# Matmuls without use behind the stages of batch 0's front end, a fold that takes high parts first, and sums of batch 1 queued behind it

## The chip, the cores and the metric

The kernel runs on one core of a Trainium2 chip. A core has TensorE (PE, matmuls; its weight loads are shown as PEld), VectorE (DVE), ScalarE (ACT), GpSimdE (POOL) and SyncE (SP, which issues most of the transfers); each works through its own queue in order and waits for the others by semaphores. The metric is the device time of one execution in microseconds. The kernel before took 1105.98 us (median of 3 runs, 1105.55 to 1107.51).

## The reference

Eight batches, each with 8 heads, 576 tokens and 64 channels a head, go through attention against keys and values that are averaged over 8 tokens each, and then through a mixing block: a Fourier transform over tokens and channels whose real part is added, a normalisation, and a two-layer network with 2048 hidden channels. Cut to what matters:

```python
k_p = k.reshape(B, H, Sp, 8, D).mean(axis=3)
v_p = v.reshape(B, H, Sp, 8, D).mean(axis=3)
attn = softmax((q @ k_p.T) / sqrt(D))          # per batch and head
x = (attn @ v_p).transpose(0, 2, 1, 3).reshape(B, S, H * D)
mixed = np.real(np.fft.fft(np.fft.fft(x, axis=1), axis=2))
u = x + mixed
un = (u - mean(u)) / sqrt(var(u) + 1e-06)
out = u + np.maximum(un @ w_ch1, 0.0) @ w_ch2
```

## The kernel before

For each batch `b` the generator `fe(b)` (L231 to L656) makes the front end: attention, transform and normalisation. `ffn` (L661) makes the two-layer network for a block of columns. Most precise products are made of three: a value is split into a high part and a low part, and high times high, low times high and high times low are added in PSUM.

**Batch 0's front end, in order.** Head pairs are taken in the order 3, 2, 0, 1. For a pair `g`: sums of the keys (L259 on VectorE for batch 0), copies of them into `kpb` (L268, L269), scores into PSUM tiles `psS` (L327, three column groups and then two), maximum and subtraction on VectorE (L329, L338), exponential on ScalarE (L340), sum and reciprocal on VectorE (L341 to L343), the product with it on GpSimd (L344). Then come transposes into `psT`, `psV` and `psR` (L365, L375, L376, L386), copies out of them on ScalarE (L368, L380, L390), and the values `psX` (L408). For pairs 3 and 2 ScalarE copies psX to `X` (L410 to L415); for pairs 0 and 1 VectorE adds and subtracts it (L418, L419).

**The transform.** The even channels are folded on VectorE to `tmpE` (L484), ScalarE rounds that to the high part `eh` (L477), and VectorE subtracts to get the low part `el` (L478; both are shown as `f`). One row is folded apart: GpSimd writes `xt` (L490), ScalarE its high part into `xe` (L493), VectorE its low part (L494). The odd channels give `tmpO` (L496). Then come three products `psA` (L517), each of seven records: `eh` by the high constants twice, `el` by the high constants twice, `eh` by the low constants twice, and `xe`. They are copied out in two parts (L501, L502 and L505 to L523). `psB` (L533, eighteen records) does the same for the odd channels; `psQ` and `psP` (L550) transform over the tokens; L556 to L583 add the results on VectorE; `psM` (L596) gives the mean that L600 subtracts; L590 and L591 split the outcome into `unh` and `unl`, the operands of the first FFN product `g` (L687).

**PSUM.** There are eight banks: `g1` and `fe` with two each, `acc0` to `acc3`. `bank` (L217) gives batch 0 the banks of the FFN, in turn g1, acc0, g1, acc1, acc2, acc3; the other batches use `fe`. The FFN takes g1 for its first product and acc0 to acc3 for its second.

**Weights.** They come as pieces of 512 KB (numbers 0 to 33, the last four half as large; the first 24 are w1 and w2 in turn). `prep_w` (L175) makes a piece's high part (`wd`, then L199) and its low part (L200), on ScalarE (L190, L192), VectorE (L194, L195), ScalarE and GpSimd; the low part is written to DRAM (L201) and read again for each FFN step (L210). When a piece is prepared, the place in which it lay takes the load of a later one (L202). Piece 4's first ScalarE operations are queued behind batch 0's last copy of `psB` (L189).

**Order.** The program is traced in the order of the generators (L707 on): batch 0's front end up to the mark "z", eleven weight pieces, batch 1 with the rest of batch 0 and the first steps of batch 2, then FFN blocks with the other batches between. A scheduler with a timing model then fixes each engine's queue; what it takes to be ready sooner stands further ahead. So batch 1's and the weights' operations stand between batch 0's in every queue. `tc.issue_after(ins)` queues what its block traces on the engine of `ins` behind `ins`; it is an order of issue, not a wait. Buffers have tags with a number of slots: `k` (one slot) holds batch 1's keys of one pair, and also `xt`; `v` and `vs` hold batch 1's values of one pair and their sums; `w` (seven slots) the weights in work and the low parts.

Of the kernel before, what the change touches and what calls it, by code (L numbers as in the profile page):

```python
# [8 lines left out]
F32 = mybir.dt.float32  # L9
# [5 lines left out]
ALU = mybir.AluOpType  # L15
# [7 lines left out]
P = 128  # L23
# [29 lines left out]

TAIL0, TAIL1, NEXT, STEPS = 10, 11, 20, 10
E0, O0, E1, O1 = 0, 1, 2, 3

HEADS = [(0, 1), (2, 3), (5, 4), (7, 6)]
GROUPS = [(3, 2), (0, 1)]
# [17 lines left out]
def raw(ap):  # L76
    return ap.bitcast(F32)
# [3 lines left out]
def tile_kernel(ctx: ExitStack, tc: tile.TileContext, qt, kt, vm, vr, w1, w2, cad, cbd, mkd, out):  # L81
# [93 lines left out]
    def prep_w(n):  # L175
        if n >= len(pieces):
            return
        i, f, c, w, _ = pieces[n]
        cl = slice(c * P, (c + w) * P)
        if wide:  # L180
            st = staged.pop(n)
            hi = st[:, :, :, 1]
            halves = st.bitcast(U16)
            d0 = wk.tile([P, DM], I32, tag="w", bufs=7, name="wd")[:, 0:w * P]
            di = d0.rearrange("p (c m) -> p c m", m=P)
            dh = d0.bitcast(U16).rearrange("p (c m h) -> p c m h", m=P, h=2)
            d0 = d0.bitcast(F32)

            with tc.issue_after(behind["B", 0].ins) if n == 4 else ExitStack():  # L189
                nc.scalar.activation(hi.bitcast(F32), hi.bitcast(F32), AF.Copy, scale=REBIAS)  # L190

                nc.scalar.activation(dh[:, :, :, 0], st.bitcast(U8)[:, :, :, 3], AF.Copy, scale=1.0 / 32.0, bias=-15.5 / 32.0)  # L192

            nc.vector.tensor_scalar(out=dh[:, :, :, 1], in0=halves[:, :, :, 3], scalar1=0x8000, scalar2=None, op0=ALU.bitwise_and)  # L194
            nc.vector.scalar_tensor_tensor(out=di, in0=hi, scalar=3, in1=di, op0=ALU.logical_shift_left, op1=ALU.bitwise_or)  # L195
        else:
            d0 = staged.pop(n)
        wh = high(i, f)[:, cl]
        nc.scalar.copy(out=wh, in_=d0)  # L199
        nc.gpsimd.tensor_tensor(out=d0, in0=d0, in1=raw(wh), op=ALU.subtract)  # L200
        nc.sync.dma_start(wls[i][:, f, cl], d0)  # L201
        for m in after.get(n, ()):  # L202
            load_w(m)
# [10 lines left out]

    turn, behind = [0], {}

    def bank(b, name, late=False):  # L217
        tag = "fe"
        if b == 0 and not late:
            tag = ["g1", "acc0", "g1", "acc1", "acc2", "acc3"][turn[0] % 6]  # L220
            turn[0] += 1
        return pp.tile([P, 512], F32, tag=tag, bufs=2 if tag in ("fe", "g1") else 1, name=name)

# [2 lines left out]

    def tt(name, dt=F32):
        return wk.tile([P, 5 * W2J], dt, tag="t", bufs=2, name=name)


    def fe(b):  # L231
# [24 lines left out]
        def total(out, src, pool):  # L256

            if b not in pool:
                nc.vector.tensor_reduce(out=out, in_=src, op=ALU.add, axis=AX.X)  # L259
                return  # L260
            for n in (4, 2, 1):
                nc.gpsimd.tensor_tensor(out=out if n == 1 else src[:, :, 0:n], in0=src[:, :, 0] if n == 1 else src[:, :, 0:n], in1=src[:, :, 1] if n == 1 else src[:, :, n:2 * n], op=ALU.add)  # L262
# [49 lines left out]
        def scores(gi, i):  # L312
# [10 lines left out]
            for c0, n in ((0, 3), (3, 2)):  # L323
                ps = bank(b, f"psS{b}_{g}_{c0}")
                for c in range(n):
                    r0 = SROW[c0 + c]
                    nc.tensor.matmul(ps[:, c * W2J:(c + 1) * W2J], lhsT=q[:, r0:r0 + P], rhs=kpb[g % 2], start=True, stop=True)  # L327
                pv = ps[:, 0:n * W2J].rearrange("p (c h j) -> p c h j", h=2, j=J)
                nc.vector.tensor_reduce(out=mx[:, c0:c0 + n], in_=pv, op=ALU.max, axis=AX.X, negate=(b, g) in SM)  # L329
                if (b, g) in SM:  # L330
                    nm = mx[:, c0:c0 + n]
                    nc.vector.tensor_scalar(out=nm, in0=nm, scalar1=1.0 / 64.0, scalar2=None, op0=ALU.mult)
                    for c in range(n):
                        for h in range(2):
                            x = (slice(None), c0 + c, slice(h, h + 1))
                            nc.scalar.activation(t[:, c0 + c, h], pv[:, c, h], AF.Exp, scale=1.0 / 64.0, bias=mx[x], accum_out=sm[x])
                else:
                    nc.vector.tensor_tensor(out=t[:, c0:c0 + n], in0=pv, in1=mx[:, c0:c0 + n].unsqueeze(3).broadcast_to([P, n, 2, J]), op=ALU.subtract)  # L338
# [17 lines left out]
        def transposes(gi):  # L356
# [3 lines left out]
            for i, g in enumerate(pairs):  # L360
                t = st["t", g]
                ah, al = gt(2 * i, "ah"), gt(2 * i + 1, "al")
                ps = bank(b, f"psT{b}_{g}")
                for c in range(4):
                    nc.tensor.transpose(out=ps[:, c * P:(c + 1) * P], in_=t[:, c, 0:P], identity=ident)  # L365
                if b in NAT:
                    ah = raw(ah)
                nc.scalar.copy(out=ah[:, 0:512], in_=ps)  # L368
                if b not in NAT:
                    nc.vector.tensor_tensor(out=al[:, 0:512], in0=ps, in1=raw(ah[:, 0:512]), op=ALU.subtract)  # L370
                a[g] = (ah, al)
# [11 lines left out]
            rem = [(512, S, ps[0:32, 2 * P + 64:3 * P])]  # L383
            ps2 = bank(b, f"psR{b}_{gi}")
            for c in range(4):
                nc.tensor.transpose(out=ps2[0:32, c * P:(c + 1) * P], in_=rt[:, c], identity=ident)  # L386
            rem.append((0, 512, ps2[0:32, :]))
            for a0, a1, src in rem:
                if b in NAT:
                    nc.scalar.copy(out=raw(R[0:32, a0:a1]), in_=src)  # L390
# [7 lines left out]
        def values(g):  # L398
            ah, al = st["a"][g]
            wh, wl = st["w", g]  # L400
            for cl in halves:
# [3 lines left out]
                else:  # L405
                    mm = [(wh, ah[:, cl]), (wl, ah[:, cl]), (wh, al[:, cl]), (rw[g in (1, 2)], st["R"][0:96, cl])]
                for i, (w, a) in enumerate(mm):
                    nc.tensor.matmul(ps, lhsT=w, rhs=a, start=(i == 0), stop=(i == len(mm) - 1))  # L408
                if g == 3:
                    nc.scalar.copy(out=Xb[:, O0, cl], in_=ps)  # L410
                    nc.scalar.copy(out=Xb[0:1, E1, cl], in_=ps[0:1])
# [63 lines left out]
        def split(dst, src, n):  # L475
            eh, el = [gt(i, "f").rearrange("p (g s) -> p g s", g=2)[:, :, 0:n] for i in dst]
            nc.scalar.copy(out=eh, in_=src)  # L477
            eng.tensor_tensor(out=el, in0=src, in1=raw(eh), op=ALU.subtract)  # L478
            return eh, el

        Xe = Xb.rearrange("p (g t) s -> p t g s", t=2)
# [9 lines left out]
        nc.scalar.copy(out=xt[:, 0:HS + 1:HS], in_=o0[:, 0:S:HS])  # L491
        nc.scalar.copy(out=xt[:, HS + 1:HS + 2], in_=o0[:, HS:HS + 1])
        nc.scalar.copy(out=xe[0:1], in_=xt)  # L493
        nc.vector.tensor_tensor(out=xe[32:33], in0=xt, in1=raw(xe[0:1]), op=ALU.subtract)  # L494
        tmp = tt("tmpO").rearrange("p (g s) -> p g s", g=2)[:, :, 0:HS]
        behind["O", b] = (nc.vector if b == 0 else nc.gpsimd).tensor_tensor(out=tmp, in0=Ov[:, :, 0:HS], in1=Ov[:, :, HS:S], op=ALU.subtract)  # L496
        yield
# [10 lines left out]

        AB = [gt(0, "A0"), gt(1, "A1"), None, None, gt(4, "AB2")]
        A2, B2 = AB[4][:, 0:258], AB[4][:, 258:514]  # L510
        for i, m in enumerate((P, P, 34)):
            s0 = i * P
            ps = bank(b, f"psA{b}_{i}")[0:m, 0:258]
            mm = [(x[:, j, s0:s0 + m], cc[:, j, y]) for x, y in ((eh, 0), (el, 0), (eh, 1)) for j in range(2)]
            mm.append((xe[:, s0:s0 + m], xc))
            for n, (w, a) in enumerate(mm):
                nc.tensor.matmul(ps, lhsT=w, rhs=a, start=(n == 0), stop=(n == len(mm) - 1))  # L517
            if i < 2:
                parts((AB[i],), ps, 258)
            else:  # L520
# [72 lines left out]
        for cl in halves:  # L593
            ps = bank(b, f"psM{b}")[:, 0:HS]
            if b in NM:
                nc.tensor.matmul(ps, lhsT=raw(avg), rhs=s_[:, cl], start=True, stop=True)  # L596
            else:
                nc.tensor.matmul(ps, lhsT=avg, rhs=sh[:, cl], start=True, stop=False)
                nc.tensor.matmul(ps, lhsT=avg, rhs=sl[:, cl], start=False, stop=True)
# [288 lines left out]
```

## Time and profile before

| | |
|---|---|
| runs shown | 1105.98 us median, 1105.55 to 1107.51 |
| profiled execution, its own time | 1103.99 us |
| its span, first to last instruction | 1102.2 us |
| mean granted TensorE clock | 0.978 |
| TensorE busy | 1048.4 us (95%) |
| VectorE busy | 615.1 us (56%) |
| ScalarE busy | 415.6 us (38%) |
| GpSimd busy | 249.6 us (23%) |
| moved by DMA | 175.79 MB, mean 159 GB/s |

Times in the profile are microseconds from the span's start. A row of the timeline gives start, length, engine, line of the kernel, operation, written and read tiles, shapes, and how many records it merges; in brackets stands how long the engine stood idle before it, and what ended that. A merged row's length reaches to the end of its last record, which overlaps the next row, so what a matmul costs is read from one start to the next. A float32 product leaves two records, a product of rounded parts one. The page's forty slices give each engine's busy share in tenths. Seven tenths of the chain of work that ended last are the FFN's two products:

```profile
PE acc L671 35%; PE g L687 35%; PE psX L408 3%; PE psS L327 2%; PE psA L517 2%; PE psP L550 2%; PE psB L533 1%; PE psQ L550 1%; PE psT L365 1%; DMA k<-in_kt 1%; DMA wst<-in_w 1%; DVE unl L591 1%; DVE acc L701 0%; PE psR L386 0%; DVE X L600 0%
```

### The profile page before, as it was taken

The numbers are of one execution on the slowest core, as the hardware profiler recorded it, in microseconds if no ns is written. First come the engines' busy times: TensorE is split into PE (matmuls) and PEld (weight loads), VectorE is DVE, ScalarE is ACT, GpSimd is POOL, SyncE is SP. The second block draws the span as 40 slices with busy tenths as digits, with TensorE's granted clock in tenths as the row PEclk, the third lists the DMA queues.
The fourth block names the chain that finished last, engine by engine and source line by source line (L and its number), as shares of the span: only waits on it lengthen the run. The fifth ranks groups of instructions, "written<-read, shape, count | busy, mean of one in ns | idle before, by whom it ended". The sixth has DMA issues, their size and how long they took to land.

```text
span 1102.2 us, 17441 instructions
## 1 busy us (share of the span) xinstructions
PE 1048.4 (95%) x6484; PEld 1009.0 (92%) x6484; DVE 615.1 (56%) x1237; ACT 415.6 (38%) x1102; POOL 249.6 (23%) x249
## 2 busy tenths in 40 slices
PE   6659988999999999999999999999998999999997
PEld 5447878999999999999999999999997999999997
DVE  7597877845386464754467454755547544532122
ACT  5678754443144331533324332433314422221110
POOL 4463355212140032200331111500323000400000
PEclk9768999999999999999999999999999999999999
DMA  6759977655345454444534444435534334346563
GB/s 219 266 185 304 314 256 226 202 175 172 115 118 157 134 162 126 126 140 153 155 110 137 146 139 147 131 113 172 161 95 127 96 106 125 106 124 186 167 186 98
DMA packets 91877, 175.79 MB, mean 159 GB/s; under 512 B 10128, under 2 KB 17296, under 8 KB 91536
## 3 DMA queue, kind: packets, MB, share of 16 engines
q1 hardware_dynamic: 91504, 172.01, 50.8%
q0 software_dynamic: 288, 2.66, 0.6%
q8 instruction: 51, 0.84, 0.3%
q14 instruction: 34, 0.28, 0.1%
HBM read 156.81 MB, written 17.83 MB: 158 GB/s over the span
## 4 chain that ended last, share of the span: by engine, by line
PE 83%; DVE 4%; DMA 2%; ACT 1%; issue 1%; POOL 1%; SPq 0%; DVEq 0%; POOLq 0%; ACTq 0%
PE acc L671 35%; PE g L687 35%; PE psX L408 3%; PE psS L327 2%; PE psA L517 2%; PE psP L550 2%; PE psB L533 1%; PE psQ L550 1%; PE psT L365 1%; DMA k<-in_kt 1%; DMA wst<-in_w 1%; DVE unl L591 1%; DVE acc L701 0%; PE psR L386 0%; DVE X L600 0%
## 5 line engine op out<-in xcount | busy, mean ns | idle before, releaser
L692 DVE SCALAR_TENSOR_TENSOR hl<-g,hh 128x384 fp32r<-128x384 f32 (+1 forms) x208 | 108.5, 522 | 209.9 <-ACT hh L691 208.8
L691 ACT ACTIVATE hh<-g 128x384 fp32r<-128x384 f32 (+1 forms) x208 | 96.5, 464 | 325.6 <-PE g L687 313.8
L671 PE MATMUL acc<-hh,w2h 128*128 128x384 f32 (+1 forms) x832 | 190.2, 329 | 3.4 <-ACT hh L691 2.8
L671 PE MATMUL acc<-hh,w2low 128*128 128x384 f32 (+1 forms) x832 | 186.5, 326 | 0.1
L671 PE MATMUL acc<-hl,w2h 128*128 128x384 f32 (+1 forms) x832 | 181.5, 327 | 2.8 <-DVE hl L692 2.8
L687 PE MATMUL g<-unh,w1low 128*128 128x384 f32 (+1 forms) x832 | 179.0, 330 | 2.8 <-DMA w1low<-w1l 2.7
L687 PE MATMUL g<-unl,w1h 128*128 128x384 f32 (+1 forms) x832 | 177.6, 330 | 3.8 <-DVE unl L591 3.4
L687 PE MATMUL g<-unh,w1h 128*128 128x384 f32 (+1 forms) x832 | 175.9, 329 | 2.7 <-ACT unh L590 2.7
L671 PEld LDWEIGHTS acc<-hh,w2h 128*128 128x128 f32 x832 | 142.6, 189 | 5.9 <-ACT hh L691 3.7
L687 PEld LDWEIGHTS g<-unl,w1h 128*128 128x128 f32 x832 | 141.6, 191 | 6.5 <-DVE unl L591 5.0
L687 PEld LDWEIGHTS g<-unh,w1low 128*128 128x128 f32 x832 | 141.0, 191 | 5.3 <-DMA w1low<-w1l 4.0
L687 PEld LDWEIGHTS g<-unh,w1h 128*128 128x128 f32 x832 | 139.9, 190 | 5.6 <-ACT unh L590 4.0
L671 PEld LDWEIGHTS acc<-hl,w2h 128*128 128x128 f32 x832 | 140.8, 189 | 4.2 <-DVE hl L692 3.5
L671 PEld LDWEIGHTS acc<-hh,w2low 128*128 128x128 f32 x832 | 143.4, 188 | 0.6 <-DMA w2low<-w2l 0.3
L344 POOL TENSOR_TENSOR t<-t,sm 128x720 f32<-128x720 f32 x32 | 49.3, 1540 | 284.9 <-DVE sm L343 267.3
L262 POOL TENSOR_TENSOR k<-k 128x288 f32<-128x288 f32 (+1 forms) x56 | 36.7, 656 | 98.4 <-DMA k<-in_kt 85.3
L582 POOL TENSOR_TENSOR U<-X,U 128x576 f32<-128x576 f32 (+1 forms) x14 | 19.3, 1380 | 128.1 <-DVE X L566 128.1
L327 PE MATMUL psS<-kpb,q 128*128 128x144 f32 x280 | 42.7, 287 | 2.5 <-DVE X L600 2.4
L327 PEld LDWEIGHTS psS<-kpb,q 128*128 128x128 f32 x280 | 39.4, 190 | 3.1 <-DVE X L600 2.6
L329 DVE TENSOR_REDUCE mx<-psS 128x6 f32<-128x432 f32 x64 | 33.1, 524 | 12.9 <-PE psS L327 12.8
L340 ACT ACTIVATE t<-t 128x720 f32<-128x720 f32 x30 | 24.1, 805 | 33.7 <-DVE t L338 33.5
L341 DVE TENSOR_REDUCE sm<-t 128x10 f32<-128x720 f32 x30 | 26.9, 898 | 12.9 <-ACT t L340 12.6
(207 smaller groups left out, 1420.2 us busy)
## 6 DMA issues: line engine op xcount, KB each, us to landing
w1low<-w1l SPq DMA_DIRECT2D x208, 256.0 KB, 2.6
w2low<-w2l SPq DMA_DIRECT2D x208, 256.0 KB, 2.8
wst<-in_w SPq DMA_DIRECT2D x30, 512.0 KB, 4.7
q<-in_qt SPq DMA_DIRECT2D x28, 288.0 KB, 3.1
k<-in_kt SPq DMA_DIRECT2D x28, 288.0 KB, 2.9
v<-in_vm SPq DMA_DIRECT2D x28, 256.0 KB, 3.3
out<-U SPq DMA_DIRECT2D x18, 384.0 KB, 3.5
w1l<-wd SPq DMA_DIRECT2D x16, 256.0 KB, 4.9
```

The lines of the kernel that those rows point to most:

```text
L262: nc.gpsimd.tensor_tensor(out=out if n == 1 else src[:, :, 0:n], in0=src[:, :, 0] if n == 1 else src[:, :, 0:n], in1=src[:, :, 1] if n == ...
L327: nc.tensor.matmul(ps[:, c * W2J:(c + 1) * W2J], lhsT=q[:, r0:r0 + P], rhs=kpb[g % 2], start=True, stop=True)
L329: nc.vector.tensor_reduce(out=mx[:, c0:c0 + n], in_=pv, op=ALU.max, axis=AX.X, negate=(b, g) in SM)
L340: nc.scalar.activation(t, t, AF.Exp, scale=1.0 / 64.0)
L341: nc.vector.tensor_reduce(out=sm, in_=t, op=ALU.add, axis=AX.X)
L344: ins = nc.gpsimd.tensor_tensor(out=t, in0=t, in1=sm.unsqueeze(3).broadcast_to([P, 5, 2, J]), op=ALU.mult)
L408: nc.tensor.matmul(ps, lhsT=w, rhs=a, start=(i == 0), stop=(i == len(mm) - 1))
L550: nc.tensor.matmul(ps, lhsT=w, rhs=a, start=(i == 0), stop=(i == 6))
L671: nc.tensor.matmul(acc[e], lhsT=w[:, e], rhs=h, start=(f == f0 and x == 0), stop=(f == f1 - 1 and x == 2))
L687: nc.tensor.matmul(ps, lhsT=w[:, c], rhs=x[:, ti, cl], start=(n == 0), stop=(n == 11))
L691: nc.scalar.activation(hh, ps, AF.Relu)
L692: nc.vector.scalar_tensor_tensor(out=hl, in0=ps, scalar=0.0, in1=raw(hh), op0=ALU.max, op1=ALU.subtract)
```

## The change

There are five edits.

1. `keep_busy(n, ins)` issues n products of the identity with itself into a PSUM tile `idle`, queued behind the matmul `ins`. Nothing reads the result. They stand at the start (8), behind the second score tile of each pair (3, 7, 9 and 4 for pairs 3, 2, 0 and 1), behind pair 3's transposes (3), behind the second `psR` (4), behind pair 1's values (12), between the two parts of `psA` (3), and behind the second `psM` (8). All are in batch 0's front end.
2. `idle` holds the bank acc3, so `bank` gives batch 0 other turns: seven places with `fe` among them for the first 24 tiles, then five.
3. `psA`'s records are put in the order `eh` by high, `eh` by low, `el` by high, `xe`; for batch 0 the four with `eh` are issued for all three tiles first, then the rest.
4. In batch 0 the low part of `xe` (L494) is queued behind the low part of the fold (L478).
5. On VectorE the sums of batch 1 (values and remainders, L259) and weight piece 3 (L194, on which L195 hangs) are queued behind the low part of batch 0's fold.

```diff
+BUSY = {"start": 8, "S3": 3, "S2": 7, "S0": 9, "S1": 4, "T3": 3, "R": 4, "X": 12, "A": 3, "M": 8}
...
-            nc.vector.tensor_scalar(out=dh[:, :, :, 1], in0=halves[:, :, :, 3], scalar1=0x8000, scalar2=None, op0=ALU.bitwise_and)
+            with tc.issue_after(behind["E", 0].ins) if n == 3 else ExitStack():
+                nc.vector.tensor_scalar(out=dh[:, :, :, 1], in0=halves[:, :, :, 3], scalar1=0x8000, scalar2=None, op0=ALU.bitwise_and)
...
+    idle = pp.tile([P, 512], F32, tag="acc3", name="idle")
+
+    def keep_busy(n, ins=None):
+
+        with tc.issue_after(ins.ins) if ins else ExitStack():
+            for _ in range(n):
+                nc.tensor.matmul(idle[:, 0:P], lhsT=ident, rhs=ident, start=True, stop=True)
+
     def bank(b, name, late=False):
         tag = "fe"
         if b == 0 and not late:
-            tag = ["g1", "acc0", "g1", "acc1", "acc2", "acc3"][turn[0] % 6]
+
+            tags = ["g1", "acc0", "fe", "g1", "acc1", "acc2", "fe"] if turn[0] < 24 else ["g1", "acc0", "g1", "acc1", "acc2"]
+            tag = tags[turn[0] % len(tags)]
             turn[0] += 1
...
+    keep_busy(BUSY["start"])
...
             if b not in pool:
-                nc.vector.tensor_reduce(out=out, in_=src, op=ALU.add, axis=AX.X)
+
+                with tc.issue_after(behind["E", 0].ins) if b == 1 else ExitStack():
+                    nc.vector.tensor_reduce(out=out, in_=src, op=ALU.add, axis=AX.X)
                 return
...
-                    nc.tensor.matmul(ps[:, c * W2J:(c + 1) * W2J], lhsT=q[:, r0:r0 + P], rhs=kpb[g % 2], start=True, stop=True)
+                    mm = nc.tensor.matmul(ps[:, c * W2J:(c + 1) * W2J], lhsT=q[:, r0:r0 + P], rhs=kpb[g % 2], start=True, stop=True)
+                if b == 0 and c0:
+                    keep_busy(BUSY[f"S{g}"], mm)
...
+                if b == 0 and g == 3:
+                    keep_busy(BUSY["T3"], mm)
...
+            if b == 0 and gi:
+                keep_busy(BUSY["R"], mm)
...
+                if b == 0 and g == 1 and cl.start:
+                    keep_busy(BUSY["X"], last)
...
-            eng.tensor_tensor(out=el, in0=src, in1=raw(eh), op=ALU.subtract)
+            behind["f", b] = eng.tensor_tensor(out=el, in0=src, in1=raw(eh), op=ALU.subtract)
...
-        nc.vector.tensor_tensor(out=xe[32:33], in0=xt, in1=raw(xe[0:1]), op=ALU.subtract)
+        with tc.issue_after(behind["f", 0].ins) if b == 0 else ExitStack():
+            nc.vector.tensor_tensor(out=xe[32:33], in0=xt, in1=raw(xe[0:1]), op=ALU.subtract)
+            behind["E", b] = behind["f", b]
...
-        for i, m in enumerate((P, P, 34)):
+        def channels(i, m, part):
             s0 = i * P
-            ps = bank(b, f"psA{b}_{i}")[0:m, 0:258]
-            mm = [(x[:, j, s0:s0 + m], cc[:, j, y]) for x, y in ((eh, 0), (el, 0), (eh, 1)) for j in range(2)]
+            if part == 0:
+                st["A", i] = bank(b, f"psA{b}_{i}")[0:m, 0:258]
+            ps = st["A", i]
+            mm = [(x[:, j, s0:s0 + m], cc[:, j, y]) for x, y in ((eh, 0), (eh, 1), (el, 0)) for j in range(2)]
             mm.append((xe[:, s0:s0 + m], xc))
-            for n, (w, a) in enumerate(mm):
-                nc.tensor.matmul(ps, lhsT=w, rhs=a, start=(n == 0), stop=(n == len(mm) - 1))
+            for n, (w, a) in list(enumerate(mm))[4 * part:4 + 4 * part]:
+                last = nc.tensor.matmul(ps, lhsT=w, rhs=a, start=(n == 0), stop=(n == len(mm) - 1))
+            return ps, last
+
+        shares = (P, P, 34)
+        if b == 0:
+
+            for i, m in enumerate(shares):
+                _, last = channels(i, m, 0)
+            keep_busy(BUSY["A"], last)
+        for i, m in enumerate(shares):
+            if b:
+                channels(i, m, 0)
+            ps, _ = channels(i, m, 1)
...
-                nc.tensor.matmul(ps, lhsT=raw(avg), rhs=s_[:, cl], start=True, stop=True)
+                last = nc.tensor.matmul(ps, lhsT=raw(avg), rhs=s_[:, cl], start=True, stop=True)
+                if b == 0 and cl.start:
+                    keep_busy(BUSY["M"], last)
```

More of the change, by code (lines that the diff above doesn't have):

```diff
@@ L364, in transposes @@
                 for c in range(4):
-                    nc.tensor.transpose(out=ps[:, c * P:(c + 1) * P], in_=t[:, c, 0:P], identity=ident)
+                    mm = nc.tensor.transpose(out=ps[:, c * P:(c + 1) * P], in_=t[:, c, 0:P], identity=ident)
+                if b == 0 and g == 3:
+                    keep_busy(BUSY["T3"], mm)
                 if b in NAT:
@@ L385, in transposes @@
             for c in range(4):
-                nc.tensor.transpose(out=ps2[0:32, c * P:(c + 1) * P], in_=rt[:, c], identity=ident)
+                mm = nc.tensor.transpose(out=ps2[0:32, c * P:(c + 1) * P], in_=rt[:, c], identity=ident)
             rem.append((0, 512, ps2[0:32, :]))
+            if b == 0 and gi:
+                keep_busy(BUSY["R"], mm)
             for a0, a1, src in rem:
@@ L407, in values @@
                 for i, (w, a) in enumerate(mm):
-                    nc.tensor.matmul(ps, lhsT=w, rhs=a, start=(i == 0), stop=(i == len(mm) - 1))
+                    last = nc.tensor.matmul(ps, lhsT=w, rhs=a, start=(i == 0), stop=(i == len(mm) - 1))
+                if b == 0 and g == 1 and cl.start:
+                    keep_busy(BUSY["X"], last)
                 if g == 3:
```

## The prediction

> **What bounds the kernel now.** I read the page's forty slices first, for the place where TensorE is not full. One slice is 27.6 us.
>
> ```profile
> PE   6659988999999999999999999999998999999997
> PEclk9768999999999999999999999999999999999999
> ```
>
> After slice 6 TensorE is full at full clock, so a microsecond saved there is a microsecond of matmul work and the change touches none of it. Before slice 4 it is neither full nor at full clock: this is batch 0's front end, alone at first. So the windows of this stretch come next (columns: PE, PEld, DVE, ACT, POOL busy, granted clock, DMA share, GB/s; a row with one busy number is PE alone).
>
> ```profile
> 8.00:18.00 10.00, 7.21 (x28) 1.00 0.97 360
> 30.00:32.00 2.00, 0.25 (x3) 1.00 1.00 408
> 32.00:34.00 2.00, 1.52 (x4) 0.50 0.99 385
> 34.00:36.00 2.00, 2.00 (x9) 0.64 1.10 350
> ...
> 44.00:56.00 12.00, 10.35 (x39) 0.50 0.44 138
> 66.00:90.00 24.00, 13.55 (x44) 0.50 0.57 178
> ...
> 10.00:20.00 10.00, 8.01 (x32) 7.11 (x32) 9.67 (x20) 6.01 (x17) 1.95 (x4) 1.00 0.81 295
> 60.00:80.00 20.00, 8.70 (x42) 6.81 (x41) 19.64 (x42) 14.18 (x46) 13.65 (x11) 0.65 0.58 193
> 100.00:130.00 30.00, 28.04 (x187) 24.27 (x186) 24.22 (x54) 24.45 (x63) 13.12 (x12) 1.00 0.97 326
> ```
>
> The clock stands at half from 44 to 56 and from 66 to 90 us, while PE has work. The clock of 1.00 at 8 to 18 us can't be believed: the timeline of PE (start, length) shows there the same matmuls at twice the length they have later.
>
> ```profile
> 12.43 2.77 PE L327 MATMUL psS<-kpb,U 128*128 128x144 f32 x10 [0.61 <-ACT kpb L269]
> 16.58 2.74 PE L327 MATMUL psS<-kpb,U 128*128 128x144 f32 x10 [1.38 <-DVE t L338]
> 19.21 1.12 PE L365 MATMUL psT<-ident,t 128*128 128x128 f32 x4
> ...
> 28.94 0.66 PE L365 MATMUL psT<-ident,t 128*128 128x128 f32 x4
> 29.43 0.27 PE L375 MATMUL psV<-ident,t 128*128 128x128 f32 x1
> ...
> 44.10 1.66 PE L517 MATMUL psA<-ca,f 128*128 128x258 f32 x6 [5.30 <-ACT f L477]
> 46.90 1.23 PE L517 MATMUL psA<-ca,f 128*128 128x258 f32 x4 [1.14 <-DVE f L478]
> 48.05 0.58 PE L517 MATMUL psA<-ca,xe 33*128 33x258 f32 x1
> ...
> 51.23 0.42 PE L517 MATMUL psA<-ca,xe 33*34 33x258 f32 x1
> 52.06 4.11 PE L533 MATMUL psB<-ca,f 128*128 128x256 f32 x18 [0.41 <-ACT f L477]
> 56.01 1.39 PE L327 MATMUL psS<-kpb,q 128*128 128x144 f32 x10
> ...
> 78.03 1.33 PE L687 MATMUL g<-unh,w1h 128*128 128x288 f32 x4 [2.65 <-ACT unh L590]
> ```
>
> Ten score records take 2.74 us at 16.58 and 1.39 at 56.01. So PE runs at half speed up to about 25 us as well; before the first recorded change the column means nothing. But speed counts only where PE is what others wait for. The waits of PE up to 92 us (total, times, longest) say where it is not:
>
> ```profile
> PE psS L327 <- ACT kpb L269: 6.9, 3, 5.5
> PE psT L365 <- POOL t L344: 5.4, 2, 4.5
> PE psA L517 <- ACT f L477: 5.3, 1, 5.3
> ```
>
> In the scores, PE waits for the others, and VectorE is busy 9.67 of 10 us at 10 to 20. The place where PE's own time is the path is the fold into psA and psB, 44 to 56 us. What holds psA back is VectorE's queue:
>
> ```profile
> 39.45 0.45 DVE L194 TENSOR_SCALAR wd<-wst 128x512 uint16<-128x512 uint16 x1
> 39.80 0.43 DVE L418 TENSOR_TENSOR X<-psX,X 128x288 f32<-128x288 f32 x1
> ...
> 40.88 0.67 DVE L259 TENSOR_REDUCE vs<-v 128x64 f32<-128x512 f32 x1
> 41.48 0.82 DVE L195 SCALAR_TENSOR_TENSOR wd<-wst,wd 128x512 int32<-128x512 int32 x1
> 42.23 0.44 DVE L419 TENSOR_TENSOR X<-psX,X 128x288 f32<-128x288 f32 x1
> 42.60 0.74 DVE L484 TENSOR_TENSOR tmpE<-X 128x574 f32<-128x574 f32 x1
> 43.26 0.67 DVE L259 TENSOR_REDUCE vt<-vr 32x64 f32<-32x512 f32 x1
> 43.85 0.74 DVE L496 TENSOR_TENSOR tmpO<-X 128x576 f32<-128x576 f32 x1
> 44.62 1.42 DVE L494 TENSOR_TENSOR xe<-xt,xe 1x290 fp32r<-1x290 f32 x1
> 46.08 0.76 DVE L478 TENSOR_TENSOR f<-tmpE,f 128x580 fp32r<-128x580 f32 x1
> ```
>
> Weight preparation (L194, L195) and batch 1's sums (L259) stand between batch 0's adds (L418, L419) and the fold (L484). Its low part, `f` at 46.08, stands behind vt, tmpO and xe, though its input was ready after 44 us (ScalarE's copy is what released psA at 44.10).
>
> **The change part by part**, against the profiled execution: 1103.99 us, 1102.2 of it span. Negative is a gain.
>
> **Price of a filler.** One filler is a float32 product of 128 columns; a score product of 144 columns leaves two records (ten for five), so a filler is two. At full clock four psT records of 128 columns take 29.43 - 28.94 = 0.49 us, 0.12 each: a filler costs 0.25. At half clock the scores have 19.21 - 16.58 = 2.63 us for ten, 0.26 each: 0.5. There are 8+3+7+9+4+3+4+12+3+8 = 61, so 15 us at full clock and 30 at half. Waits of 6.9, 5.4 and 5.3 us cover most of it.
>
> **Does the clock rise?** At 8 to 18 us PE was busy 7.21 of 10 and stayed slow; at 32 to 36 it was busy 3.52 of 4 and rose. So some share between 72 and 88% is wanted. From 5.5 to 22 us at half clock the fillers of S3, S2, S0, S1 and T3 (26 x 0.5 = 13 us) on top of those 72% make PE full, so it must rise; once up, the same work and fillers halve. It fell at 32, after the row 30 to 32 shows 0.25 us of work in 2: a wait of some 2 us is enough. X's 12 fillers (3.0 us) stand in the 5.3 us wait ahead of psA, which term 3 shortens by 1.7, and leave 0.6. I take it that psA and psB run at full clock. The Trainium skill, page "TensorE: Matmul & The Clock Gate", section "HAM oscillation — how this bites in real kernels", allows idle gaps of up to about 3.4 us. The row at 30 us differs: the shorter wait sufficed. By that rule psA would be warm with or without X's fillers, and the sum would be the same.
>
> **Terms.**
> 1. Scores and transposes up to 30 us: VectorE and GpSimd bind. Of PE only a psT behind each normalisation is on the path, 1.12 against 0.66, so 0.46 once or twice: -0.8 (0 to -1.5). The other bank rotation removes the 1.38 us wait at 16.58, but VectorE is full behind it: 0.
> 2. psX of the last two groups, 32 to 39 us, half cold: -1.0; R's four fillers (1.0) can stand ahead of it. I take -0.5 (-1.0 to +0.4).
> 3. VectorE before the fold: L194, L259 and L195 leave, by starts 0.35 + 0.60 + 0.75: -1.7 (-1.0 if the adds then wait for psX). Moved behind: batch 1's sums feed its values, which PE takes behind the first FFN matmuls (78.03 us), and weight piece 3 the second FFN step; more than 30 us hide that, and if they didn't it would cost the 0.67 us of a sum. Their SyncE orders (next loads of v, writing of the low part) can hold the queue; that is in term 6.
> 4. psA. Now 44.10 to 51.65 = 7.55 us. After: twelve high records at the pitch of half clock (48.05 - 46.90)/4 = 0.29, halved 0.14: 1.7 us. Beside them the low part on VectorE, 0.76, then xe, 1.42: 2.2 us from the start. A's fillers (0.75) end at 2.5, then nine records by 0.14: 3.7. Gain -3.8 (at half clock 3.5 + 1.5 + 2.6 = 7.6: nothing).
> 5. psB: 56.01 - 52.06 = 3.95 us with the last bit at full clock; eighteen at psA's 0.14, 2.5 us: -1.45, rounded to -1.5 (0 if cold).
> 6. Between psB and the first FFN matmul VectorE is busy 19.64 of 20 us (60 to 80), with batch 1 and weights between. These must come earlier too. Weight pieces from number 4 are queued behind psB's copy (L189), so they do. Batch 1's first k load needs the buffer of `xt`, which xe reads last: it is issued at 46.17, right after xe's end.
>
> ```profile
> 46.17 0.38 SPq L241 DMA_DIRECT2D k<-in_kt  x1
> ```
>
> psA starts at 44.10 - 3.0 = 41.1 by terms 1 to 3, xe ends 2.2 us later, at 43.3 against 46.04: batch 1's loads move by 2.7 us, batch 0 by 8.3. Where batch 1's operations stand ahead of batch 0's in a queue (psS at 56.01 ahead of psQ), batch 0 waits up to 4.7 us: +2.0, between 0 and that. psM's eight fillers stand where PE is busy 13.55 of 24 us (66 to 90) and cost nothing, or their 2 to 4 us if that gap were gone; they don't fill it, so the first FFN step stays cold as now.
> 7. Behind 90 us: the PE waits from 92 to 240 us (hh, hl, w1low) are in-order waits for weights.
>
> ```profile
> PE acc L671 <- ACT hh L691: 2.8, 3, 1.4
> PE acc L671 <- DVE hl L692: 2.5, 2, 2.3
> PE g L687 <- DMA w1low<-w1l: 2.3, 2, 1.5
> ```
>
> I take 0 for their change (-2 to +3).
>
> Sum: -0.8 - 0.5 - 1.7 - 3.8 - 1.5 + 2.0 = **-6.3**, so 1097.7 for the profiled execution. The shown runs' median, 1105.98, lies 2.0 above it: **1099.7**. Ends of the terms: -1.5 - 1.0 - 1.7 - 3.8 - 1.5 - 2 = -11.5 (1094.5) and 0 + 0.4 - 1.0 - 3.8 - 1.5 + 4.7 + 3 = +1.8 (1107.8).
>
> **Rivals.**
> *A, slower: fillers at half clock ahead of real work.* If the clock doesn't rise, S2's seven take 3.5 us ahead of the scores at 12.43, where PE waits 0.6: +2.9, and S0's nine run past the transpose at 19.21: +0.5. R's four: +2.0. X's twelve take 6.0 against a wait of 5.3 less 1.7: +2.4. Terms 4 and 5 vanish, term 3 stays: +6.1, **1112**. It decides if psS and psT still take 2.7 and 1.1 us up to 22 us. For it: 72% busy was not enough at 8 to 18 us. Against it: at half clock the fillers make PE full by the sum above. Chance 0.08. The Trainium skill, the same page, section "What's actually happening", speaks for A: it asks for about 3.4 us of sustained work before the clock rises, which a group of 3 or 4 fillers alone is not; the rows agree that scattered work isn't enough.
> *B, absorbed.* From 100 to 130 us the DMA share is 0.97. If weights then come no earlier, FFN begins sooner and its waits for hh and hl grow by nearly what the front end gained: **1105.5**, half a microsecond under the median. For it: term 7's rows. Against: from 44 to 56 us the share is 0.44, and weights from number 4 move with psB. Chance 0.11.
> *C, more.* Batch 1 follows fully, term 6 is 0 or less and the terms reach their near ends: **1094.5**. Chance 0.10.
> *D, the fillers don't act where they stand.* They only are queued behind a matmul; if the next real work follows before the clock notices, only term 3 remains, 1105.98 - 1.7: **1104.3**. Chance 0.05.
>
> **How the numbers follow.** Forecast 0.66 at 1099.7, own range 1095 to 1103.5. Two tenths of a per cent, 2.2 us, is about what can be told from no change here. Forecast and C are faster: 0.76; B and D the same: 0.16; A slower: 0.08. The range reaches from a little beyond C, 1092, to the terms' far end, 1107.8, and leaves out A and the tail of C.
>
> **What would show it.** In the changed profile: psS at 9 to 17 us near 1.4 us, psT near 0.66 (the clock, terms 1, 2); no L194 or L259 of weights and batch 1 between L418 and L484, `f` right behind ScalarE's copy (3); psA from first to last under 4 us, psB about 2.5 (4, 5); first FFN matmul at 70 to 73 us in place of 78.03 (6); PE's waits from 84 to 235 us still near 10 us (7). I am wrong if psA stays cold, if psQ waits for batch 1, or if waits for hh and hl grow by what the front end gains.

## The result: as fast as forecast or faster, but for another reason

The changed kernel takes 1095.98 us (median of 5 runs, 1095.05 to 1097.22), the kernel before 1105.55 (5 runs, 1102.25 to 1107.51): ratio 0.9907, 95% interval 0.9889 to 0.9924. Its profiled execution took 1095.98 us, 1094.2 of it span, 8.0 less than before.

The forecast was 1099.7, faster, by a quicker front end of batch 0. The front end did become quicker where the forecast said, up to about 50 us. That gain was gone before the first FFN block ended. What the runs measure was won mainly at 810 to 845 us, where batch 6's front end is used, by a side effect of one edit.

### Where the time went

The page of the changed kernel, its forty slices (27.4 us each):

```profile
PE   8848898999999999999999999999999999999997
PEclk9968999999999999999999999999999999999999
```

Slices 0 and 1 are fuller than before (88 against 66), the fillers among that work; slices 2 and 3 are not (48 against 59). The difference that lasts stands much further on: slice 30 (counted from 0), which holds 827 to 854 us of the kernel before, was an 8 and is a 9 now. The timeline of TensorE in the changed kernel (start, length; `idle` is a filler):

```profile
1.79 3.78 PE L227 MATMUL idle<-ident 128*128 128x128 f32 x16 [1.79 <-POOL ident masks.py:199]
5.97 1.50 PE L345 MATMUL psS<-kpb,U 128*128 128x144 f32 x10 [0.40 <-ACT kpb L287]
...
29.50 0.77 PE L385 MATMUL psT<-ident,t 128*128 128x128 f32 x4 [2.15 <-POOL t L364]
...
41.23 1.70 PE L547 MATMUL psA<-ca,f 128*128 128x258 f32 x12 [0.92 <-ACT f L503]
42.77 0.83 PE L227 MATMUL idle<-ident 128*128 128x128 f32 x6
43.36 0.97 PE L547 MATMUL psA<-ca,f 128*128 128x258 f32 x6
44.25 0.62 PE L547 MATMUL psA<-ca,xe 33*128 33x258 f32 x3
44.80 1.82 PE L575 MATMUL psB<-ca,f 128*128 128x256 f32 x12
47.43 0.89 PE L575 MATMUL psB<-ca,f 128*32 128x256 f32 x6 [0.81 <-DVE A L530]
...
64.30 2.29 PE L638 MATMUL psM<-s,avg 128*128 128x288 f32 x4 [5.98 <-DVE s L617]
...
76.94 2.03 PE L731 MATMUL g<-unh,w1h 128*128 128x288 f32 x7
```

The first scores take 1.50 us for ten records, so the clock is up by 6 us. psA takes 3.64 us, from 41.23 to 44.87, where it took 7.55. psB ends at 48.32 instead of 56.17: 7.9 us won. Then the gain melts: psM starts at 64.30 against 67.44, the first FFN matmul at 76.94 against 78.03.

To follow it further, I gave each TensorE record other than a filler the usual distance between starts for its shape (median behind 200 us) and added these along the queue. Both kernels do 992.3 us of such work. Changed minus before, at the moment when both have done the same amount, is the lag of the changed kernel (negative where it is ahead):

```
own work done, us    20     30     50    120    400    600    700    780    950
after              -7.8   -2.5   +2.7   +2.2   +2.0    0.0   +0.1   -8.0   -8.0
```

So the front end's 7.8 us became a loss of some 2 us by 50 us of work (about 115 us of time). Up to 120 the lag swings, from about +3 at 70 to about -3 at 100, since the two kernels wait at different places there; from 120 on it stands at about +2. These 2 us come back before 600. The rest of the gain lies between 700 and 780. There the kernel before has these gaps on TensorE, and VectorE has this work (timelines):

```profile
828.27 0.90 PE L327 MATMUL psS<-kpb,q 128*128 128x144 f32 x6
831.53 0.76 PE L327 MATMUL psS<-kpb,q 128*128 128x144 f32 x4 [2.36 <-DVE X L600]
832.23 2.35 PE L687 MATMUL g<-unh,w1h 128*128 128x384 f32 x8
835.50 0.62 PE L687 MATMUL g<-unl,w1h 128*128 128x384 f32 x2 [0.92 <-DVE unl L591]
837.39 1.20 PE L687 MATMUL g<-unl,w1h 128*128 128x384 f32 x3 [1.26 <-DVE unl L591]
```

```profile
826.19 1.35 DVE L600 TENSOR_TENSOR X<-U,psM 128x1152 f32<-128x1152 f32 x1 [0.44 <-PE psM L599]
827.46 0.90 DVE L341 TENSOR_REDUCE sm<-t 128x10 f32<-128x720 f32 x1
828.28 1.95 DVE L701 TENSOR_TENSOR acc<-acc,rb 128x384 f32<-128x384 f32 x4
830.13 1.34 DVE L600 TENSOR_TENSOR X<-U,psM 128x1152 f32<-128x1152 f32 x1
...
833.97 1.48 DVE L591 TENSOR_TENSOR unl<-X,unh 128x576 fp32r<-128x576 f32 x1
```

An FFN block ends here and the next begins (behind FFN step 144; a step is the 24 matmuls of one weight column group). The next block is the first that reads batch 6's `unh` and `unl`. Batch 6's mean is subtracted (L600) only now, with the ended block's eight operations (L701, L702) and batch 7's scores between. TensorE waits, and its clock falls (granted 0.50 from 838 to 840 us). The windows of 35 us around it (busy PE, granted clock) for the kernel before and, in the second fence, the changed one:

```profile
810.00:845.00 35.00, 30.46 (x170) 0.95 0.37 113
```

```profile
810.00:845.00 35.00, 35.00 (x214) 1.00 0.47 145
```

Before: 4.5 us idle and a clock of 0.95. After: none idle and full clock. In the changed kernel batch 6's psM runs ahead of the block by three and a half FFN steps, and its mean is subtracted (L644) long before the block begins, so there is nothing to wait for:

```profile
812.98 0.30 PE L642 MATMUL psM<-s,avg 128*128 128x288 f32 x1
```

```profile
814.92 1.34 DVE L644 TENSOR_TENSOR X<-U,psM 128x1152 f32<-128x1152 f32 x1
```

Theory L (late): the new order of psA's records holds for all batches, not for batch 0 alone. It lets the scheduler put every later front end further ahead in the queues, and the stall at step 144 goes. Theory F (front): the gain is batch 0's front end, as forecast.

### The profile page after: what moved, and what is told of

Its sections match the earlier page's. It is cut to its first block, busy times and chain, and to the rows that moved or that the text cites. A ratio compares the mean times of both kernels' runs of the same rounds, so it can differ in the third digit from the quotient of the medians.

```text
span 1094.2 us, 17702 instructions
## 1 busy us (share of the span) xinstructions
PE 1050.1 (96%) x6606; PEld 1017.7 (93%) x6606; DVE 611.6 (56%) x1237; ACT 416.0 (38%) x1102; POOL 247.3 (23%) x249
## 4 chain that ended last, share of the span: by engine, by line
PE 84%; DVE 6%; DMA 4%; ACT 3%; issue 1%; POOL 1%; SPq 0%; DVEq 0%; POOLq 0%; ACTq 0%
PE acc L715 35%; PE g L731 35%; PE psX L432 3%; PE psS L345 3%; PE psA L547 2%; PE psP L592 2%; DMA wst<-in_w 1%; DMA w1low<-w1l 1%; PE psB L575 1%; PE psT L385 1%; DVE wd L199 1%; PE psQ L592 1%; DVE wd L198 1%; DMA k<-in_kt 1%; PE psR L408 1%
## 5 line engine op out<-in xcount | busy, mean ns | idle before, releaser
L364 POOL TENSOR_TENSOR t<-t,sm 128x720 f32<-128x720 f32 x32 | 45.9, 1434 | 286.7 <-DVE sm L363 248.0
L280 POOL TENSOR_TENSOR k<-k 128x288 f32<-128x288 f32 (+1 forms) x56 | 41.0, 732 | 97.6 <-DMA k<-in_kt 84.3
L349 DVE TENSOR_REDUCE mx<-psS 128x6 f32<-128x432 f32 (+1 forms) x64 | 33.1, 526 | 19.6 <-PE psS L345 19.3
L745 DVE TENSOR_TENSOR acc<-acc,rb 128x384 f32<-128x384 f32 (+1 forms) x60 | 29.0, 517 | 13.5 <-PE acc L715 13.5
```

The costliest lines, as they stand in the source:

```text
L364: ins = nc.gpsimd.tensor_tensor(out=t, in0=t, in1=sm.unsqueeze(3).broadcast_to([P, 5, 2, J]), op=ALU.mult)
L745: nc.vector.tensor_tensor(out=acc[e], in0=acc[e], in1=rb[:, cl], op=ALU.mult)
```

## The experiments

All ratios are to the kernel before, run on the same chip beside it.

### order_later: only the record order, only in batches 1 to 7

```diff
-mm = [... for x, y in ((eh, 0), (el, 0), (eh, 1)) ...]
+mm = [... for x, y in (((eh, 0), (eh, 1), (el, 0)) if b else ((eh, 0), (el, 0), (eh, 1))) ...]
```

> The kernel before, with psA's records in the new order (eh by high, eh by low, el by high) for batches 1 to 7 only; nothing of batch 0's front end is touched. Theory L (the gain is made late: the new order lets each later front end stand further ahead in the queues, so batch 6's mean is ready before its FFN block asks for it and the stall at 826 to 838 us goes): about 7 us faster than before, ratio 0.992 to 0.995; no PE gap over 0.5 us between 800 and 850 us; front end up to 92 us as before. Theory F (the gain is batch 0's front end, as forecast): within 2 us of before, ratio 0.998 to 1.002, stall still there.

Measured: 1094.79 us, ratio 0.9902 (0.9887 to 0.9917). One reordered list that batch 0 doesn't use gives the whole of the change's gain, and more than the 0.992 to 0.995 that theory L expected. TensorE is never idle in the window of the stall:

```profile
810.00:845.00 35.00, 35.00 (x214) 1.00 0.48 150
```

The lag against before is 0.0 at 20 us of own work, -1.2 at 700 and -9.0 at 780. Theory F falls.

### after_old_order: the change without that

The changed kernel with the old order for batches 1 to 7.

```diff
-mm = [... for x, y in ((eh, 0), (eh, 1), (el, 0)) ...]
+mm = [... for x, y in (((eh, 0), (el, 0), (eh, 1)) if b else ((eh, 0), (eh, 1), (el, 0))) ...]
```

> The changed kernel, with the old order of psA's records put back for batches 1 to 7; all of batch 0's edits stay. Theory L: batch 6's mean comes back to within two FFN steps of its use, the stall returns in part or whole: 3 to 9 us slower than the changed kernel, ratio to before 0.995 to 1.002. Theory F: as the changed kernel, ratio 0.989 to 0.993.

Measured: 1097.35 us, ratio 0.9930 (0.9913 to 0.9947): by the ratios some 2.5 us slower than the changed kernel, though the two intervals overlap, and well under the kernel before. Theory L's 3 to 9 us and 0.995 to 1.002 missed; the ratio alone lies at the upper end of what theory F expected. The trace is what speaks for L: between 700 and 780 us of own work this kernel gains 5.8 us, where the changed kernel gains 7.9. The waits of TensorE between 815 and 845 us show a small stall in place of the large one:

```profile
PE acc L715 <- DVE U L746: 0.6, 1, 0.6
PE g L731 <- POOL unl L633: 0.4, 1, 0.4
PE acc L715 <- DVE hl L736: 0.2, 1, 0.2
```

So batch 0's edits alone also move the later front ends, by less: batch 6's psM stands behind 142.6 FFN steps (before 143.5, changed kernel 140.5), and a lead of 1.4 steps is nearly enough. I counted this place from the trace in each run (FFN matmuls ahead of the first psM, by 24); the table stands below.

### order_all: the record order alone, in all batches

```diff
-mm = [... for x, y in ((eh, 0), (el, 0), (eh, 1)) ...]
+mm = [... for x, y in ((eh, 0), (eh, 1), (el, 0)) ...]
```

> The kernel before with the new order of psA's records for all batches, batch 0 with them, and nothing else. Theory L: as order_later, 6 to 9 us faster than before, so as good as the whole change. Theory F: 0 to 1 us faster, since psA stays at half clock and the low part still stands behind xe.

Measured: 1100.04 us (1096.60 to 1102.18), ratio 0.9948 (0.9918 to 0.9978). Faster than before, but by less than order_later, though its profiled execution (1096.60, the fastest of five) has no stall either and stands at -7.4 us. What differs in its other executions is not in that trace; this stays open.

### no_fillers: the change with one filler instead of 61

```diff
-BUSY = {"start": 8, "S3": 3, "S2": 7, "S0": 9, "S1": 4, "T3": 3, "R": 4, "X": 12, "A": 3, "M": 8}
+BUSY = {"start": 1, "S3": 0, "S2": 0, "S0": 0, "S1": 0, "T3": 0, "R": 0, "X": 0, "A": 0, "M": 0}
```

> The changed kernel with one filler (at the start) in place of 61. Theory L: the fillers win time only up to about 58 us, and it is lost again by 110 us, so within 2 us of the changed kernel, ratio to before 0.989 to 0.993. Theory F: psA, psB and the transposes fall back to half clock: 4 to 6 us slower than the changed kernel, ratio 0.994 to 0.997.

Measured: 1094.48 us, ratio 0.9903 (0.9888 to 0.9919). The fillers are worth nothing in the total. Their effect is real where they stand. Without them psA is slower (TensorE of no_fillers):

```profile
41.09 4.24 PE L547 MATMUL psA<-ca,f 128*128 128x258 f32 x18 [3.75 <-ACT f L503]
45.26 1.01 PE L547 MATMUL psA<-ca,xe 33*128 33x258 f32 x3
...
63.22 2.29 PE L638 MATMUL psM<-s,avg 128*128 128x288 f32 x4 [4.66 <-DVE s L617]
74.81 2.29 PE L731 MATMUL g<-unh,w1h 128*128 128x288 f32 x8 [2.14 <-ACT unh L632]
```

psA takes 5.2 us instead of 3.6, but psM and the first FFN matmul come no later, they come 1.1 and 2.1 us earlier: TensorE waits for VectorE and then for ScalarE there.

### push6: the stall put back

order_later with one number changed. `free` tells from which position of the program a batch may overwrite its half of U.

```diff
-free = {1: 0, 2: 64, 3: 128, 4: 160, 5: 224, 6: 256, 7: 320}
+free = {1: 0, 2: 64, 3: 128, 4: 160, 5: 224, 6: 280, 7: 320}
```

> order_later with one number changed: batch 6's second half is allowed 24 positions (twelve FFN steps) later in the program, so that its psM stands behind 143.3 FFN steps in TensorE's queue instead of 140.5 (143.5 in the kernel before); the block that needs it begins behind 144. All else, psA's order too, stays. Theory L: the stall between 820 and 845 us comes back, 6 to 9 us slower than order_later, ratio to before 0.997 to 1.001. Rival O (the new record order itself makes psA or its neighbours cheaper): stays at 0.989 to 0.993.

Measured: 1103.91 us, ratio 0.9983 (0.9967 to 0.9998). Nearly all of the gain is gone, and the same wait is back (TensorE, 815 to 845 us):

```profile
PE psS L327 <- DVE X L600: 2.4, 1, 2.4
PE g L687 <- DVE unl L591: 1.6, 2, 1.3
```

The profiled execution was the fastest of ten (1100.62). In it the lag is -3.4 at 700 us of own work and still -3.4 at 780: no gain in the place where order_later gains 7.8. The record order itself is therefore not what makes it faster; the place in the queue is.

### pull_by_sums: the stall taken away by something unrelated

The kernel before, with batch 3's value sums on GpSimd.

```diff
-PV = {0}
+PV = {0, 3}
```

> The kernel before with batch 3's value sums on GpSimd instead of VectorE, and nothing else: no part of the change. It puts batch 6's psM behind 142.6 FFN steps instead of 143.5, the same as after_old_order, and batch 4's behind 92.6 instead of 94.6 (its block begins behind 96). Theory L: most of the stall goes, 5 to 9 us faster than before, ratio 0.992 to 0.996. Rival O: no gain, 0.998 to 1.002.

Measured: 1098.58 us, ratio 0.9924 (0.9903 to 0.9946). No line of the change is in it, and it gains most of what the change gains, with the same small rest of a stall as after_old_order. The places, and TensorE's idle time in the window 810 to 845 us (35.00 less busy), of the seven kernels:

```
                  batch 4's psM    batch 6's psM    idle, us   ratio
                  (needed at 96)   (needed at 144)
before                94.6             143.5          4.5      1
fillers_only          94.6             143.5          3.9      0.9978
push6                 92.5             143.3          4.0      0.9983
after_old_order       92.1             142.6          1.2      0.9930
pull_by_sums          92.6             142.6          1.2      0.9924
after                 91.9             140.5          0.0      0.9907
order_later           92.5             140.5          0.0      0.9902
```

In these seven, idle time and gain follow the place of batch 6. The place doesn't set the whole time: order_all stands at 140.5 with no idle time in its trace and gains less, and the two lite kernels below both stand at 142.7 and are 6 us apart. Batch 4's place goes with the two us before 600 us of own work: the kernel before and fillers_only, with 94.6 against 96, have waits of 0.6, 0.4 and 0.2 us at its block (480 to 600 us), and the changed kernel and pull_by_sums have none there. No run moved batch 4 alone.

### fillers_only: what the clock alone gives

The kernel before with the fillers and the bank rotation, without the moves on VectorE, with psA in the old order. The three fillers between the parts of psA have no place there, so it has 58 of the 61.

```diff
+BUSY = {"start": 8, "S3": 3, "S2": 7, "S0": 9, "S1": 4, "T3": 3, "R": 4, "X": 12, "A": 3, "M": 8}
...
-            tag = ["g1", "acc0", "g1", "acc1", "acc2", "acc3"][turn[0] % 6]
+            tags = ["g1", "acc0", "fe", "g1", "acc1", "acc2", "fe"] if turn[0] < 24 else ["g1", "acc0", "g1", "acc1", "acc2"]
+            tag = tags[turn[0] % len(tags)]
```

> The kernel before with the 61 fillers and the bank rotation alone; VectorE's queue and psA's order as before. Batch 6's psM stays behind 143.5 FFN steps. Theory L: psA and psB are faster up to 60 us, but it is lost again by 110 us and the late stall stays: within 2 us of before, ratio 0.998 to 1.002. Theory F: terms 1, 2, 5 and a part of 4, so 3 to 5 us faster, ratio 0.995 to 0.997.

Measured: 1103.17 us, ratio 0.9978 (0.9960 to 0.9996). The value lies between the two expectations, and the interval reaches into both. A gain of 0.4 to 4.4 us is left, and the trace shows -0.9 us from 120 us of own work on. Together with no_fillers (no loss without them) I read it as small or nothing.

### after_pace, lite_after, lite_later: do the weights eat the front end's gain?

after_pace traces the weight pieces earlier among the FFN steps:

```diff
-AHEAD, LEAD, PACE = 11, 12, 0.65
+AHEAD, LEAD, PACE = 11, 12, 0.85
```

> The changed kernel with the weight pieces traced earlier among the FFN steps (PACE 0.85 for 0.65). Theory W (the front end's gain of 7.8 us at 58 us is lost because weights set the pace from 95 to 190 us): the FFN steps from 10 to 24 come 2 to 4 us sooner than in the changed kernel, total 1092 to 1094. Rival Q (it is lost in the queues ahead of the first FFN step, where batch 1's keys stand ahead of unh): no change, 1095 to 1097.

Measured: 1096.77 us, ratio 0.9913 (0.9891 to 0.9935), so no gain, as rival Q expected. In the trace it stands more than 7 us behind the kernel before at 70 us of own work: batch 1 comes earlier with it (its psM behind 16.8 steps instead of 18.3) and takes that from the FFN.

The lite kernels use w1's low part in place of w2's in the first 24 FFN steps, so that 24 loads go:

```diff
                     if (i, step + m) not in lows:
+                        if i == 1 and step + m < 24:
+                            lows[1, step + m] = lows[0, step + m]
+                            continue
                         load_low(i, step + m)
```

> The changed kernel, in which the first 24 FFN steps don't load w2's low part but use w1's in its place, so that 24 transfers of 256 KB and their buffers go. Theory W: with the weights eased, more of the front end's gain lasts: at 50 us of TensorE's own work it stands 3 us or more ahead of lite_later, and is 2 to 5 us faster in all. Rival Q: within 2 us of lite_later at that point and in all.

> order_later (the old front end) with the same loads left out as in lite_after: the measure for it. Both put batch 6's psM behind 142.7 FFN steps, so the late part should be the same in both. Theory W: 2 to 5 us slower than lite_after. Rival Q: within 2 us of it.

Measured: 1096.14 us, ratio 0.9916 (0.9894 to 0.9937), and 1102.43, 0.9974 (0.9956 to 0.9993). The totals go theory W's way, 6 us apart where it said 2 to 5, but the trace doesn't bear out its reason: lite_after is 4.2 us ahead at 50 us of own work, but both stand alike at 120 (-4.9 and -5.3), and lite_later loses its 5.7 us behind that, at later blocks (gaps of 2.6 us at 212 and 2.1 at 330 us). Leaving out loads moved the later batches too. The pair doesn't settle it.

### keys_behind_unh and keys_no_fillers: the queue ahead of the first FFN step

The timeline of ScalarE in the changed kernel shows where 5 us go between psM and the FFN:

```profile
70.17 0.25 ACT L286 COPY kpb<-ks 64x72 f32<-64x72 f32 x1 [5.34 <-POOL ks L280]
...
75.89 1.46 ACT L632 CAST unh<-X 128x288 fp32r<-128x288 f32 x4
```

ScalarE stands 5.34 us at the copy of batch 1's last keys; behind it are exponentials of batch 1 and then batch 0's `unh`, though the first half of X was ready at about 70. The edit queues that copy behind `unh`:

```diff
-                nc.scalar.copy(out=uh, in_=X[:, ti, cl])
+                behind["u", b] = nc.scalar.copy(out=uh, in_=X[:, ti, cl])
...
-            nc.scalar.copy(out=kb[0:64, 0:J], in_=ks[0:64])
-            nc.scalar.copy(out=kb[64:128, J:W2J], in_=ks[64:128])
+            with tc.issue_after(behind["u", 0].ins) if (b, g) == (1, 1) else ExitStack():
+                nc.scalar.copy(out=kb[0:64, 0:J], in_=ks[0:64])
+                nc.scalar.copy(out=kb[64:128, J:W2J], in_=ks[64:128])
```

> The changed kernel, with ScalarE's two copies of batch 1's last keys (kpb, pair 1) queued behind batch 0's copies to unh; in the changed kernel ScalarE stands 5.3 us at them, ahead of unh. Theory W (weights and their transfers set the pace from 95 us): the first FFN matmul comes 3 to 5 us sooner than 76.9 us, but FFN step 24 stands within 2 us of the changed kernel and the total stays at 1094 to 1097. Rival Q (the queue ahead of the first FFN step is what loses the front end's gain): 3 to 5 us faster in all, 1091 to 1093.

Measured: 1092.09 us, ratio 0.9875 (0.9848 to 0.9901). ScalarE and TensorE there:

```profile
71.25 1.40 ACT L633 CAST unh<-X 128x288 fp32r<-128x288 f32 x4
```

```profile
73.56 2.03 PE L732 MATMUL g<-unh,w1h 128*128 128x288 f32 x7
```

The FFN begins 3.4 us sooner, and at 400 us of own work the lag is -1.3 instead of +2.0: those 3.3 us stay. The total lies in rival Q's range, though its interval (0.9848 to 0.9901) and the changed kernel's (0.9889 to 0.9924) overlap a little. Rival Q is right in this part; of the 4.5 us by which the FFN begins sooner than in the kernel before, 3.2 are still lost by 120 us of own work. The same kernel with the fillers taken out:

```diff
-BUSY = {"start": 8, "S3": 3, "S2": 7, "S0": 9, "S1": 4, "T3": 3, "R": 4, "X": 12, "A": 3, "M": 8}
+BUSY = {"start": 1, "S3": 0, "S2": 0, "S0": 0, "S1": 0, "T3": 0, "R": 0, "X": 0, "A": 0, "M": 0}
```

> keys_behind_unh with one filler in place of 61. If fillers gain only time that batch 0 then waits for VectorE ahead of psM, it is as fast as keys_behind_unh: 1090 to 1094, ratio to before 0.985 to 0.990. If, with the queue ahead of unh mended, the clock of the front end counts, it is 3 us or more slower than keys_behind_unh: ratio 0.990 to 0.994.

Measured: 1088.85 us (1088.28 to 1093.40), ratio 0.9830 (0.9814 to 0.9846). This is the fastest kernel of the study, faster than both: its interval lies below that of the changed kernel (0.9889 to 0.9924) and of no_fillers (0.9888 to 0.9919). It is faster than both expectations. So with this copy moved, the fillers gain nothing either; the intervals with and without them (from 0.9848, to 0.9846) just don't meet. Its profiled execution was the slowest of its five (1093.40), so its trace doesn't show why the others are faster still; that stays open.

## Why the prediction was right, and where it was wrong

The time lies in the range, the direction is the forecast's, and the mean gain (9.6 us of the medians against 6.3) is of the same size. That it came out so is luck. By the trace, the changed kernel stood about 2 us behind the kernel before from 120 to 400 us of own work; the gain came at two later blocks, which the prediction left out of its sum. The time is also nearer to rival C (1094.5) than to the forecast, and C's condition, term 6 at 0 or less, was not met. Step by step:

- **The opening.** "a microsecond saved there is a microsecond of matmul work and the change touches none of it" is the step that failed. Edit 3's record order holds for every batch, and every later queue is set again by the scheduler. Nor is TensorE full behind slice 6: the row that the prediction shows has an 8 at slice 30, the stall of 4.5 us, and no term of the sum goes past 240 us. push6 and pull_by_sums show that most of the gain hangs on the place of the later front ends, batch 6's above all.
- **Clock.** Right in the outcome, warm by 6 us, and rival A didn't come. But the sum counted the fillers from S3 to T3; the eight at the start had done it before them (sixteen records in 3.78 us, and the next ten scores in 1.50). The clock fell again behind the wait of 2.15 us ahead of 29.50 (granted 0.50 from 30 to 32 us) and was back at 1.00 from 34 us, so psA and psB ran warm, as taken. Without the fillers that isn't so, where the prediction thought psA warm even without X's: in no_fillers, behind a wait of 3.75 us, psA began at a granted clock of 0.50 (41 to 45 us).
- **Term 1** (-0.8): nothing. The last transpose of the attention starts at 29.50, before at 29.54; GpSimd's product is what it waits for, as the waits had said.
- **Terms 2 and 3** (-2.2): -2.9 at psA's start, 41.23 against 44.10. No weights and no sums of batch 1 stand between the adds any more.
- **Term 4** (-3.8): -3.9; psA takes 3.64 us, 3.7 was worked out.
- **Term 5** (-1.5): -0.6; psB takes 3.52 us from first to last, before 4.11, since it waits 0.81 for VectorE's copies of psA. The 0.41 us between psA and psB are gone too. With terms 1 to 5 at -7.9 in place of -8.3, the front half was forecast well.
- **Term 6** (+2.0): mis-sized. From psB's end to the first FFN matmul +6.8 (-7.9 to -1.1), above its far end of 4.7, which doesn't follow from its own figures either (8.3 less 2.7 is 5.6). The mechanism named, operations of batch 1 and the weights ahead of batch 0's, fits the rows, but it was not psS in TensorE's queue. Of the 6.8, 4.7 are lost ahead of psM, where TensorE waits 5.98 us for VectorE (before 4.11), which is busy 15.3 of the 16.3 us from 48 to 64.3 with weights and batch 1 between; no run tested this part. The other 2.0 are lost between psM and the FFN, where the last key copy stands in ScalarE's queue; keys_behind_unh takes 3.4 us back there.
- **Term 7** (0): from the first FFN matmul to 120 us of own work another +3.3. TensorE's idle time grows by only 1.1 us of that (13.5 of 129.9 us, before 12.4 of 126.7); the mean granted clock is 0.92 there, before 0.94. The lag turns from -2.7 to +2.7 between 101 and 110 us, at one wait for w1low and the half clock behind it (granted 0.50 from 102 to 108 us; 0.89 from 100 to 130, before 1.00):

```profile
101.07 0.93 PE L731 MATMUL g<-unh,w1low 128*128 128x288 f32 x4 [1.87 <-DMA w1low<-w1l]
```

```profile
100.00:130.00 30.00, 26.60 (x160) 0.89 0.90 299
```

  For the front end alone the outcome is rival B's: order_later, fillers_only and no_fillers together show that it is worth 0 to 4 us in the total. Its path is not: the waits for hh and hl, which B said would grow, fell from 5.3 to 0.7 us, while those for the low parts of the weights rose from 2.7 to 5.6 (waits of TensorE in the changed kernel, 84 to 232 us):

```profile
PE g L731 <- DMA w1low<-w1l: 4.4, 4, 1.9
...
PE acc L715 <- DMA w2low<-w2l: 1.2, 1, 1.2
PE acc L715 <- DVE hl L736: 0.7, 1, 0.7
```

  That the weights are the cause is argued, not shown.

## What to carry to other kernels

A gain at the start of a long pipeline has to be followed to the place where the next stage begins: ask what stands ahead of the first consumer in each engine's queue before counting it. Where a scheduler lays out all queues anew, an edit works wherever its line is used, so compare the two kernels' lag along the whole run before believing the local story. A unit that other work must have ready at a block boundary needs lead there; here half an FFN step of lead cost 8 us, one and a half about 2, and three and a half nothing.

## What the runs showed of the hardware that was not expected

The same operation took very different times in different surroundings. The one-row subtraction `xe` took 1.42 us at 44.62 in the kernel before, where GpSimd ran a product (43.28 to 45.73, itself 2.45 us instead of about 1.3), and 0.45 in the changed kernel, where GpSimd was idle (VectorE):

```profile
42.01 0.45 DVE L521 TENSOR_TENSOR xe<-xt,xe 1x290 fp32r<-1x290 f32 x1
```

Two key sums on GpSimd took 1.63 us at 56.87 and 4.06 at 65.69 in the changed kernel (VectorE busy 9.09 of 10 us from 50 to 60 and 10.00 from 60 to 70), and 1.41 at 65.66 in the kernel before (VectorE busy 9.76 of 10). So a busy VectorE alone doesn't lengthen them. Beside the long pair VectorE mostly runs operations that read two tiles in SBUF (`wd<-wst,wd` of L199, `U<-X,U` of L625), beside the short one mostly such as read one (L329, L194); no run tests whether that is the cause. The first two rows are the changed kernel's, the third is of the kernel before:

```profile
56.87 1.63 POOL L280 TENSOR_TENSOR k<-k 128x288 f32<-128x288 f32 x2 [2.35 <-DMA k<-in_kt]
...
65.69 4.06 POOL L280 TENSOR_TENSOR k<-k 128x288 f32<-128x288 f32 x2 [4.46 <-DMA k<-in_kt]
```

```profile
65.66 1.41 POOL L262 TENSOR_TENSOR k<-k 128x288 f32<-128x288 f32 x2 [2.90 <-DMA k<-in_kt]
```

The lengthened pair stands directly ahead of the key copy that ScalarE waited for. And the granted clock fell behind short waits: behind a single one of 1.87 us in the changed kernel (ahead of 101.07 us), and in the kernel before behind three of 2.36, 0.92 and 1.26 us within 9 us (ahead of 837.39 us).
